# Attention by groups of four heads in 32-column array tiles, with the FFN and a hand-written order

## The chip, the cores and the metric

The kernel runs on one core of a Trainium2 chip. The metric is the device time of one execution in microseconds; the time before is the median of three runs. The profile comes from one more execution, recorded by the hardware profiler.

## The reference

The kernel computes attention with normalised queries and keys for 8 batches of 12 heads, 448 tokens and 64 channels, and then a multiplicative feed-forward network over the 3,584 tokens:

```python
q_n, k_n = rmsnorm(q, g_q), rmsnorm(k, g_k)        # over the 64 channels
scores = q_n @ k_n.transpose(0, 1, 3, 2) / sqrt(64)
attn = exp(scores - max); attn = attn / attn.sum(-1)
x = (attn @ v).transpose(0, 2, 1, 3).reshape(3584, 768)
out = (((x @ w1) * (x @ w2)) @ w3) @ w_out          # w1, w2 768x1024, w3 1024x1024, w_out 1024x768
```

Inputs and output are float32; the kernel works in bfloat16 with float32 sums. The product of w3 and w_out is formed once (W34), so that the second half of the network is one product.

## The kernel before

The unit of the attention is a pair of heads of one batch: 48 pairs. Tokens are cut into four blocks of 112. For each pair `S1_load` (L129) issues three loads on SP's queue, `S2_prep` (L143) squares q and k on POOL, sums on DVE (L151), forms the inverse root with Ln and Exp on ACT (L155, L157) and scales on DVE (L160, L167, L175), and casts v (L184). `S3_transpose_q` and `S3_transpose_k` (L189, L202) transpose on TensorE through PSUM; the transposed q is padded with zeros so that each head has its own 128 rows, half of them zero (POOL's memsets, L196 and L197).

`S4_scores` (L212) computes the scores of one head with keys on the PSUM partitions: two matmuls of 448 columns and one Exp of 896 columns on ACT (L228), twice per head. `S5_pv` (L234) takes blocks of the probabilities as weights, 112 by 112, and streams the 65 columns of v and of a column of ones: 16 matmuls per head, followed by a reciprocal and a multiplication on DVE. `S6_xT` (L259) transposes the result on TensorE into xT, 128 channels by 448 tokens.

`FFN1_chunk` (L273) runs 6 matmuls of 448 columns with w1 and 6 with w2, copies one sum on ACT (L290) and multiplies on DVE (L300). `FFN2_chunk` (L302) runs two sets of 8 matmuls of 384 columns, copies on ACT (L315) and issues two stores. `W34_chunk` (L102) forms one of eight row blocks of W34: eight transposes, each with its own copy, then two sets of 8 matmuls of 384 columns.

The order is that of the program: each engine takes its instructions in the order in which the loop over pairs (L352) issues them. The chunks of W34, FFN1 and FFN2 wait in one `chunk_queue`, and three to five are put between the steps of a pair (`nslots`, L360 to L365). The FFN of a batch enters the queue when its sixth pair is done (`tail`, L328). PSUM holds two buffers for scores (two banks each), two for `pv`, and two (`mm_psum`, L55) that the transposes, the FFN and W34 share. The weights are loaded by POOL's queue with a cast to bfloat16: w_out and w3 first, then w1 and w2 in two pieces per pair (`emit_wdma`, L97).

Of the kernel before, what the change touches and what calls it, by code (L numbers as in the profile page):

```python
# [13 lines left out]
AF = mybir.ActivationFunctionType  # L14


@with_exitstack
def kernel(
# [13 lines left out]
    nc = tc.nc  # L32

    B, H, S, D = q.shape
    NP = 112
    J = S // NP
    NPAIR = H // 2
    NPAIRS_TOTAL = B * NPAIR
    DM = moe_w1.shape[0]
    DFF = moe_w1.shape[1]  # L40
    CM = DM // 128
    CF = DFF // 128
    NH = DM // 2
# [12 lines left out]

    ident = const.tile([128, 128], BF)
    make_identity(nc, ident)

    gq_sb = const.tile([1, D], FP)  # L60
    nc.sync.dma_start(out=gq_sb, in_=g_q.unsqueeze(0))
    gk_sb = const.tile([1, D], FP)
    nc.sync.dma_start(out=gk_sb, in_=g_k.unsqueeze(0))
    gprod = const.tile([1, D], FP)
    nc.vector.tensor_tensor(out=gprod, in0=gq_sb, in1=gk_sb, op=MULT)
    gprod2 = const.tile([1, D], FP)
    nc.vector.tensor_scalar(
        out=gprod2, in0=gprod, scalar1=0.125, scalar2=None, op0=MULT
    )
    ones_row = const.tile([1, NP], FP)  # L70
    nc.vector.memset(ones_row, 1.0)
    g_bcast = const.tile([NP, D], BF)
    g_ps = mm_psum.tile([NP, D], FP, tag="mm")
    nc.tensor.matmul(out=g_ps, lhsT=ones_row, rhs=gprod2, start=True, stop=True)
    nc.vector.tensor_copy(out=g_bcast, in_=g_ps)
    eps_t = const.tile([NP, 1], FP)
    nc.vector.memset(eps_t, 1e-6)

    w1s = const.tile([128, CM, DFF], BF)
    w2s = const.tile([128, CM, DFF], BF)  # L80
    w34s = const.tile([128, CF, DM], BF)
    w3s = wstage.tile([128, CF, DFF], BF)
    w_outs = wstage.tile([128, CF, DM], BF)
    w3T = wstage.tile([128, CF, DFF], BF)

    def _load(dst, srcw, c, np_=128):
        nc.gpsimd.dma_start(
            out=dst[:, c, :],
            in_=srcw.rearrange("(c p) f -> p c f", p=np_)[:, c, :],
        )  # L90

    wdma_queue = []
    for c in range(CM):
        wdma_queue.append(lambda c=c: _load(w1s, moe_w1, c))
        wdma_queue.append(lambda c=c: _load(w2s, moe_w2, c))

    def emit_wdma(n):  # L97
        for _ in range(n):
            if wdma_queue:
                wdma_queue.pop(0)()  # L100

    def W34_chunk(fc):  # L102
        for gc in range(CF):
            tps = mm_psum.tile([128, 4, 112], BF, tag="mm")
            tview = tps.rearrange("a b c -> a (b c)")[:, 0:128]
            nc.tensor.transpose(
                tview, w3s[:, fc, gc * 128 : (gc + 1) * 128], ident
            )
            nc.vector.tensor_copy(
                out=w3T[:, gc, fc * 128 : (fc + 1) * 128], in_=tview  # L110
            )
        for nh in range(2):
            wps = mm_psum.tile([128, NH], FP, tag="mm")
            for gc in range(CF):
                nc.tensor.matmul(
                    out=wps,
                    lhsT=w3T[:, gc, fc * 128 : (fc + 1) * 128],
                    rhs=w_outs[:, gc, nh * NH : (nh + 1) * NH],
                    start=(gc == 0),
                    stop=(gc == CF - 1),  # L120
                )
            nc.scalar.copy(out=w34s[:, fc, nh * NH : (nh + 1) * NH], in_=wps)

    out_r = out.rearrange("(b p j) n -> b j p n", b=B, j=J)
    pairs = [(b, m) for b in range(B) for m in range(NPAIR)]
    st = [dict() for _ in range(NPAIRS_TOTAL)]
    xT_tiles = {}

    def S1_load(i):  # L129
        b, m = pairs[i]  # L130
        s = st[i]
        s["q_sb"] = qkv_pool.tile([NP, 2, J, D], FP, tag="q", name="q_sb")
        s["k_sb"] = qkv_pool.tile([NP, 2, J, D], FP, tag="k", name="k_sb")
        s["v_sb"] = qkv_pool.tile([NP, 2, J, D], FP, tag="v", name="v_sb")
        for t_sb, src in ((s["q_sb"], q), (s["k_sb"], k), (s["v_sb"], v)):
            nc.sync.dma_start(
                out=t_sb.rearrange("p hh j d -> p hh (j d)"),
                in_=src[b, 2 * m : 2 * m + 2].rearrange(
                    "hh (p j) d -> p hh (j d)", j=J
                ),  # L140
            )

    def S2_prep(i):  # L143
        s = st[i]
        q_sb, k_sb, v_sb = s["q_sb"], s["k_sb"], s["v_sb"]
        sq = att_pool.tile([NP, 2, 2, J, D], BF, tag="sq")
        nc.gpsimd.tensor_tensor(out=sq[:, 0], in0=q_sb, in1=q_sb, op=MULT)  # L147
        nc.gpsimd.tensor_tensor(out=sq[:, 1], in0=k_sb, in1=k_sb, op=MULT)  # L148
        ssq = att_pool.tile([NP, 2, 2, J], BF, tag="ssq")
        with nc.allow_low_precision(reason="ssq in bf16 is fine"):  # L150
            nc.vector.tensor_reduce(  # L151
                out=ssq, in_=sq, axis=mybir.AxisListType.X, op=ADD
            )
        lnv = att_pool.tile([NP, 2, 2, J], FP, tag="lnv")
        nc.scalar.activation(out=lnv, in_=ssq, func=AF.Ln, bias=eps_t, scale=1.0 / D)  # L155
        alpha = att_pool.tile([NP, 2, 2, J], FP, tag="alpha")
        nc.scalar.activation(out=alpha, in_=lnv, func=AF.Exp, scale=-0.5)  # L157
        s["alpha"] = alpha
        qtmp = att_pool.tile([NP, J, 2, D], BF, tag="qtmp")
        nc.vector.tensor_tensor(  # L160
            out=qtmp.transpose([0, 2, 1, 3]),
            in0=q_sb,
            in1=alpha[:, 0].unsqueeze(3).broadcast_to([NP, 2, J, D]),
            op=MULT,
        )
        qs = att_pool.tile([NP, J, 2, D], BF, tag="qs")
        nc.vector.tensor_tensor(  # L167
            out=qs,
            in0=qtmp,
            in1=g_bcast.unsqueeze(1).unsqueeze(1).broadcast_to([NP, J, 2, D]),  # L170
            op=MULT,
        )
# [16 lines left out]
    def S3_transpose_q(i):  # L189
# [3 lines left out]
        for j in range(J):  # L193
            nc.tensor.transpose(qT_ps[:, j, :], qs[:, j], ident[0:NP, 0:NP])  # L194
# [216 lines left out]
```

## Time and profile before

| | |
|---|---|
| time, median of 3 runs | 608.8 us (601.33 to 610.04) |
| span of the profiled execution | 605.5 us; it is the only time on its page |
| TensorE matmuls (PE) | busy 502.2 us, 83% of the span |
| ACT | busy 368.6 us, 61% |
| DVE | busy 320.4 us, 53% |
| POOL | busy 166.4 us, 27% |

The busy time of PE counts each matmul from its start to its modelled end, and matmuls follow each other before they end; how fast they follow one another is read from the chain of waits, where a run of matmuls has its true length.

### The profile page before, as it was taken

What the parts mean: (1) busy time and instruction counts of PE and PEld (TensorE: products, weight loads), DVE (VectorE), ACT (ScalarE), POOL (GpSimd) and SP (SyncE); (2) the same over time, 40 slices, a digit from 0 to 9 for tenths busy, and PEclk for the clock granted to TensorE, in tenths of its full rate; (3) what the DMA queues carried; (4) which work ended last, traced back from release to release, by engine and by line L of the source; (5) the groups of instructions that cost most, each with busy time, mean ns of one, the idle gap of its engine ahead of it and who ended that gap; (6) DMA issues with size and microseconds to landing.
All of it is one profiled execution on the core that took longest, in us unless ns stands there. A gap on an engine that the chain in (4) does not pass through costs nothing. (4 is left out here: it accounts for less than half of the span.)

```text
span 605.5 us, 10322 instructions
## 1 busy us (share of the span) xinstructions
PE 502.2 (83%) x3970; PEld 343.9 (57%) x3970; DVE 320.4 (53%) x757; ACT 368.6 (61%) x520; POOL 166.4 (27%) x267
## 2 busy tenths in 40 slices
PE   0366787989878887899888987899978887999897
PEld 0244454746665566656665565656665566767655
DVE  0546655986456555655356544756446544643120
ACT  0367346785677775765577676865667776545322
POOL 3674222432223222322223222423223211100000
PEclk9977899999968998889878899989968998899899
DMA  9997111422423123222332123312423123001103
GB/s 198 249 238 163 45 47 31 122 67 75 137 58 92 47 80 110 86 62 66 108 87 85 54 69 114 93 62 64 140 58 92 47 59 94 17 1 47 47 0 92
DMA packets 46725, 51.53 MB, mean 85 GB/s; under 512 B 3668, under 2 KB 44116, under 8 KB 46676
## 3 DMA queue, kind: packets, MB, share of 16 engines
q1 hardware_dynamic: 42756, 44.05, 24.8%
q0 software_dynamic: 3920, 6.82, 6.1%
q8 instruction: 31, 0.51, 0.3%
q14 instruction: 18, 0.15, 0.1%
HBM read 46.66 MB, written 11.01 MB: 95 GB/s over the span
## 5 line engine op out<-in xcount | busy, mean ns | idle before, releaser
L228 ACT ACTIVATE attnT<-scp 112x896 bf16<-112x896 f32 x192 | 167.9, 917 | 58.3 <-PE scp L221 56.9
L243 PE MATMUL pv<-v_aug,attnT 112*112 112x65 bf16 x1536 | 113.6, 227 | 23.3 <-ACT attnT L228 23.3
L243 PEld LDWEIGHTS <-attnT 112*112 112x112 bf16 x1536 | 109.1, 146 | 41.1 <-ACT attnT L228 26.5
L221 PE MATMUL scp<-qsT_pad,ksT 128*112 128x448 bf16 x384 | 112.9, 404 | 23.1 <-ACT attnT L228 22.7
L308 PE MATMUL po<-w34s,abT 128*112 128x384 bf16 x512 | 89.4, 329 | 0.0
L293 PE MATMUL pb<-xTb,w2s 128*128 128x448 bf16 x336 | 79.9, 378 | 0.0
L282 PE MATMUL pa<-xTb,w1s 128*128 128x448 bf16 x336 | 77.8, 370 | 0.3
L300 DVE TENSOR_TENSOR abT<-pb,a_sb 128x448 bf16<-128x448 f32 x64 | 39.8, 622 | 66.8 <-PE pb L293 45.3
L308 PEld LDWEIGHTS <-abT 128*112 128x112 bf16 x512 | 65.6, 131 | 16.2
L221 PEld LDWEIGHTS <-ksT 128*112 128x112 bf16 x384 | 47.7, 146 | 44.1 <-ACT attnT L228 23.0
L290 ACT CAST a_sb<-pa 128x448 bf16<-128x448 f32 x64 | 33.9, 530 | 61.7 <-PE pa L282 61.1
L151 DVE TENSOR_REDUCE ssq<-sq 112x16 bf16<-112x1024 bf16 x48 | 58.1, 1213 | 25.2 <-POOL sq L148 23.9
L148 POOL TENSOR_TENSOR sq<-k_sb 112x512 bf16<-112x512 f32 x48 | 52.6, 1095 | 56.4 <-DMA k_sb<-in_k_dram 55.6
L147 POOL TENSOR_TENSOR sq<-q_sb 112x512 bf16<-112x512 f32 x48 | 51.8, 1079 | 57.4 <-DVE ssq L151 47.0
L315 ACT COPY o_sb<-po 112x384 f32<-112x384 f32 x64 | 30.0, 480 | 58.1 <-PE po L308 58.1
L155 ACT ACT_TABLE_LOAD x44 | 56.5, 1283 | 10.9 <-DVE ssq L151 9.1
L293 PEld LDWEIGHTS <-w2s 128*128 128x128 bf16 x384 | 39.8, 104 | 40.9 <-issue 9.7
L196 POOL MEMSET qsT_pad<- 64x448 bf16 x48 | 22.4, 466 | 123.6 <-PE scp L221 90.6
L282 PEld LDWEIGHTS <-w1s 128*128 128x128 bf16 x384 | 37.3, 103 | 33.4 <-issue 7.3
L160 DVE TENSOR_TENSOR qtmp<-q_sb,alpha 112x512 bf16<-112x512 f32 x48 | 33.2, 692 | 34.5 <-ACT alpha L157 34.5
L198 DVE COPY qsT_pad<-qT_ps 64x448 bf16<-64x448 bf16 x48 | 18.2, 379 | 61.5 <-PE qT_ps L194 61.5
L194 PE MATMUL qT_ps<-ident,qs 112*128 112x112 bf16 x192 | 20.4, 226 | 32.7 <-DVE qs L167 19.8
(45 smaller groups left out, 496.5 us busy)
## 6 DMA issues: line engine op xcount, KB each, us to landing
q_sb<-in_q_dram SPq DMA_DIRECT2D x48, 224.0 KB, 2.6
k_sb<-in_k_dram SPq DMA_DIRECT2D x48, 224.0 KB, 2.8
v_sb<-in_v_dram SPq DMA_DIRECT2D x48, 224.0 KB, 3.0
out_dram<-o_sb SPq DMA_DIRECT2D x64, 168.0 KB, 2.2
w3s<-in_moe_w_dram POOLq DMA_DIRECT2D x8, 256.0 KB, 11.3
w_outs<-in_moe_w_out_dram POOLq DMA_DIRECT2D x1, 1536.0 KB, 15.5
w1s<-in_moe_w_dram POOLq DMA_DIRECT2D x6, 256.0 KB, 7.3
w2s<-in_moe_w_dram POOLq DMA_DIRECT2D x6, 256.0 KB, 8.1
```

The lines of the kernel that those rows point to most:

```text
L147: nc.gpsimd.tensor_tensor(out=sq[:, 0], in0=q_sb, in1=q_sb, op=MULT)
L148: nc.gpsimd.tensor_tensor(out=sq[:, 1], in0=k_sb, in1=k_sb, op=MULT)
L151: nc.vector.tensor_reduce(out=ssq, in_=sq, axis=mybir.AxisListType.X, op=ADD)
L155: nc.scalar.activation(out=lnv, in_=ssq, func=AF.Ln, bias=eps_t, scale=1.0 / D)
L221: nc.tensor.matmul(out=scp[:, u, 0:S], lhsT=ksT[:, 2 * t + u, :], rhs=qsT_pad[:, hh].rearrange("d j p -> d (j p)"), start=True, stop=True,)
L228: nc.scalar.activation(out=attnT[:, hh, 2 * t : 2 * t + 2, :], in_=scp[:, :, 0:S], func=AF.Exp,)
L243: nc.tensor.matmul(out=pv[:, jq, :], lhsT=attnT[:, hh, jk, jq * NP : (jq + 1) * NP], rhs=v_aug[:, jk, hh, :], start=(jk == 0), stop=(jk == ...
L282: nc.tensor.matmul(out=pa, lhsT=w1s[:, c, fi * 128 : (fi + 1) * 128], rhs=xT_b[:, c, :], start=(c == 0), stop=(c == CM - 1),)
L290: nc.scalar.copy(out=a_sb, in_=pa)
L293: nc.tensor.matmul(out=pb, lhsT=w2s[:, c, fi * 128 : (fi + 1) * 128], rhs=xT_b[:, c, :], start=(c == 0), stop=(c == CM - 1),)
L300: nc.vector.tensor_tensor(out=abT[:, fi, :], in0=pb, in1=a_sb, op=MULT)
L308: nc.tensor.matmul(out=po, lhsT=abT[:, fi, j * NP : (j + 1) * NP], rhs=w34s[:, fi, nh * NH : (nh + 1) * NH], start=(fi == 0), stop=(fi == ...
```

## The change

The kernel is rewritten around the same computation.

- A unit of attention is four heads (a quad, 24 of them). Keys come in blocks of 128: three full blocks per head, and the last 64 keys of two heads share a block, so a quad has seven units (`NU`), each with one Exp of 128 partitions by 896 columns on ACT.
- `qk_exp` computes a unit with eight matmuls of 448 columns: each uses 64 rows and 32 columns of the array (`tile_position`), so no zero padding is needed.
- `pv_set` takes v (32 of its 64 channels) as the weights, 128 rows by 32 columns, for four heads side by side, and streams the probabilities, 448 columns. The result is xT itself, so `S6_xT` is gone. A third set with ones as the weights gives the sums; ACT turns them into reciprocals by Ln and Exp, and DVE multiplies.
- `narrow` replaces each 128-column matmul of FFN1, FFN2 and W34 by four matmuls with 32 columns of weights each, which stream the same columns.
- FFN2 works on token blocks of 128 over two batches (7 blocks of 896 tokens), and DVE copies its result.
- The squares move from POOL to ACT for all quads (`N_SQ_ACT = 24`). One table set with Ln, Exp, Square and copies is loaded once.
- q and k of quads 0 to 4 are transposed on TensorE, those of quads 5 to 23 by a DMA transpose on SP's queue, two per quad.
- v is loaded by POOL's queue with a cast to bfloat16, four DMAs per quad; the q and k loads are cut in two along the partitions.
- `mm_psum` has four buffers; `pv` shares them.
- The order is written out in slots of two units (84 of them): scores, one set of `pv`, a share of the FFN queue, transposes, and the preparation of later quads at slots given by tables. Filling matmuls of zeros (`warm`) run at the start. The steps of W34 lie in slots 1 to 13, and the FFN of a batch is queued after its third quad.

```diff
...
-    NP = 112
-    NPAIR = H // 2
+    NP = 128
+    J = -(-S // NP)
+    NF = S // NP
+    REST = S - NF * NP
+    SPLIT = REST * J
+    NU = 2 * NF + 1
+    HQ = 4
+    NQB = H // HQ
+    NQ = B * NQB
...
+    qkT_pool = ctx.enter_context(tc.tile_pool(name="qkT", bufs=3))
     att_pool = ctx.enter_context(tc.tile_pool(name="att", bufs=2))
+    sc_psum = ctx.enter_context(tc.tile_pool(name="sc_ps", bufs=2, space=PSUM))
+    mm_psum = ctx.enter_context(tc.tile_pool(name="mm_ps", bufs=4, space=PSUM))
...
+    N_PE_T = 5
+    N_SQ_ACT = 24
+    W34_EV = 'DA'
+    W34_NARROW = True
+    WARM = (16, 2, 11, 3, 5, 0)
+    LAG = 8
+    UNITS = 3.0
+    V_COST = 0.4
+    V_AHEAD = 2
+    MOVE = 2
+    LOADS_0 = ['w0', 'w3', 'w1', 'o0', 'w2']
+    LOADS_1 = ['w4', 'v0', 'w7', 'w6', 'w5', 'v1', 'o1', 'v2']
+    GATE = ('q', 2)
+    QK1_AT = 0
+    SHIFT = [0, -1, -1, -1, -3, -3, -3]
+    PREP_1 = {'sq0': -3, 'red0': -6, 'sq1': -6, 'red1': -3, 'alpha': -8, 'sc0': -3, 't0': -2, 'sc1': -2, 't1': 0}
+    PREP = {'load': -7, 'sq0': -5, 'red0': -5, 'sq1': -4, 'red1': -4, 'alpha': -3, 'sc0': -3, 't0': -1, 'sc1': -2, 't1': -1}
+    W34_SLOTS = {1: 2, 2: 1, 3: 2, 4: 3, 5: 1, 6: 1, 7: 3, 8: 1, 9: 1, 10: 2, 11: 2, 12: 3, 13: 2}
...
+                for p0, p1, nj, t0, t1 in halves:
+                    eng.dma_start(
+                        out=t_sb[p0:p1, h0 : h0 + n, 0:nj, :].rearrange(
+                            "p h j d -> p h (j d)"
+                        ),
+                        in_=src[b, HQ * m + h0 : HQ * m + h0 + n, t0:t1].rearrange(
+                            "h (p j) d -> p h (j d)", j=nj
+                        ),
+                    )
...
+    def prep_sq(i, pr, on_act=False):
+        s = st[i]
+        if pr == 0:
+            s["ssq"] = prep_pool.tile([NP, 2, HQ, J], FP, tag="ssq", name="ssq")
+        sq = prep_pool.tile([NP, 2, 2, J, D], FP, tag="sq", name="sq")
+        s["sq", pr] = sq
+        hs = slice(2 * pr, 2 * pr + 2)
+        for t, src in enumerate((s["q"], s["k"])):
+            if on_act:
+                nc.scalar.activation(out=sq[:, t], in_=src[:, hs], func=AF.Square)
+            else:
+                nc.gpsimd.tensor_tensor(
+                    out=sq[:, t], in0=src[:, hs], in1=src[:, hs], op=MULT
                 )
...
+        qks = prep_pool.tile([NP, 2, J, 2, D], BF, tag="qks", name="qks")
         nc.vector.tensor_tensor(
+            out=qks[:, 0],
             in0=qtmp,
+            in1=g_b.unsqueeze(1).unsqueeze(1).broadcast_to([NP, J, 2, D]),
             op=MULT,
         )
         nc.vector.tensor_tensor(
+            out=qks[:, 1].transpose([0, 2, 1, 3]),
+            in0=s["k"][:, hs],
+            in1=alpha[:, 1, hs].unsqueeze(3).broadcast_to([NP, 2, J, D]),
             op=MULT,
         )
+        if pe:
+            s["qks", pr] = qks
+        else:
+            issued.add(("t", i, pr))
+            nc.sync.dma_start_transpose(
+                out=s["qkT"][:, pr].rearrange("d t (j p) -> d (t j) p", p=NP),
+                in_=qks.rearrange("p t j h d -> p (t j h d)"),
+            )
+    def prep_pe_transpose(i, pr):
+        s = st[i]
+        issued.add(("t", i, pr))
+        qks = s.pop(("qks", pr))
+        ps = mm_psum.tile([128, 2, S], BF, tag="mm", name="qkT_ps")
+        for t in range(2):
+            for j in range(J):
+                n = NP if j < NF else REST
+                nc.tensor.transpose(
+                    ps[:, t, j * NP : j * NP + n], qks[0:n, t, j], ident[0:n, 0:n]
+                )
+        nc.vector.tensor_copy(out=s["qkT"][:, pr, :, 0:S], in_=ps)
+    def qk_exp(n):
+        i, g = divmod(n, NU)
+        s = st[i]
+        if g == 0:
+            s["P"] = p_pool.tile([NP, HQ, NF, S], BF, tag="P", name="P")
+            s["Pr"] = p_pool.tile([NP, 2, S], BF, tag="Pr", name="Pr")
+        qkT = s["qkT"]
+        sc = sc_psum.tile([NP, 2, 512], FP, tag="sc", name="sc")
+        for c0 in range(0, NP, 32):
+            if g < 2 * NF:
+                pr, blk = divmod(g, NF)
+                k0 = blk * NP + c0
+            else:
+                pr = c0 // REST
+                k0 = NF * NP + c0 % REST
+            assert ("t", i, pr) in issued
             for u in range(2):
                 nc.tensor.matmul(
+                    out=sc[c0 : c0 + 32, u, 0:S],
+                    lhsT=qkT[u * D : (u + 1) * D, pr, 1, k0 : k0 + 32],
+                    rhs=qkT[u * D : (u + 1) * D, pr, 0, 0:S],
                     start=True,
                     stop=True,
+                    tile_position=(u * D, c0),
                 )
+        if g < 2 * NF:
+            dst = s["P"][:, 2 * pr : 2 * pr + 2, blk, :]
+        else:
+            dst = s["Pr"]
+        nc.scalar.activation(out=dst, in_=sc[:, :, 0:S], func=AF.Exp)
+    def pv_set(i, kind):
+        s = st[i]
+        b, m = divmod(i, NQB)
+        ps = mm_psum.tile([128, S], FP, tag="mm", name="pv")
+        for j in range(J):
+            for h in range(HQ):
+                if kind:
+                    w = s["v"][:, h, j, (kind - 1) * HALF : kind * HALF]
+                else:
+                    w = ones[:, 0 if j < NF else 1 + h // 2, :]
                 nc.tensor.matmul(
+                    out=ps[h * HALF : (h + 1) * HALF, :],
+                    lhsT=w,
+                    rhs=s["P"][:, h, j, :] if j < NF else s["Pr"][:, h % 2, :],
+                    start=(j == 0),
+                    stop=(j == J - 1),
+                    tile_position=(0, h * HALF),
                 )
+        if kind == 0:
+            s["r"] = att_pool.tile([128, S], FP, tag="r", name="r")
+            nc.scalar.activation(out=s["r"], in_=ps, func=AF.Ln)
+            nc.scalar.activation(out=s["r"], in_=s["r"], func=AF.Exp, scale=-1.0)
+            return
+        if b not in xT:
+            xT[b] = x_pool.tile([128, CM, S], BF, tag="xT", name="xT")
         nc.vector.tensor_tensor(
+            out=xT[b][:, 2 * m + kind - 1, :], in0=ps, in1=s["r"], op=MULT
+        )
+        if kind == 2:
+            s.clear()
+            if m == NQB - 1:
+                push_ffn(b)
+    def narrow(ps, n, lhsT, rhs, start, stop):
+        for h in range(4):
+            nc.tensor.matmul(
+                out=ps[32 * h : 32 * h + 32, 0:n],
+                lhsT=lhsT[:, 32 * h : 32 * h + 32],
+                rhs=rhs,
+                start=start,
+                stop=stop,
+                tile_position=(0, 32 * h),
+            )
...
+    def ffn1_a(b, fi):
+        ps = mm_psum.tile([128, 512], FP, tag="mm", name="pa")
+        for c in range(CM):
+            narrow(
+                ps, S, w1s[:, c, fi * 128 : (fi + 1) * 128], xT[b][:, c, :],
+                c == 0, c == CM - 1,
+            )
+        a_sb = ffn_pool.tile([128, S], BF, tag="a_sb", name="a_sb")
+        nc.scalar.copy(out=a_sb, in_=ps[:, 0:S])
+        a_tiles[b, fi] = a_sb
...
+        for fi in range(CF):
+            narrow(
+                ps, NH, abT[bp][:, fi, t * 128 : (t + 1) * 128],
+                w34s[:, fi, nh * NH : (nh + 1) * NH], fi == 0, fi == CF - 1,
+            )
...
+    def push_ffn(b):
+        assert not wq
+        for fi in range(CF):
+            fillers.append(lambda b=b, fi=fi: ffn1_a(b, fi))
+            fillers.append(lambda b=b, fi=fi: ffn1_b(b, fi))
+        bp, odd = divmod(b, 2)
+        for t in range(3, 7) if odd else range(3):
+            for nh in range(2):
+                fillers.append(lambda bp=bp, t=t, nh=nh: ffn2(bp, t, nh))
...
+        nc.scalar.preload_act_table_set("natural_log_exp_and_others")
...
+        for t in range(max(todo) + 1):
+            if t == QK1_AT:
+                load_qk(1)
+            mine = agenda.pop(t, [])
...
+            for n in range(2 * t, min(2 * t + 2, NQ * NU)):
+                qk_exp(n)
...
+            old = len(fillers)
+            for i, kind in todo.get(t, []):
+                pv_set(i, kind)
+            for n, part in mine:
+                if part == "v":
+                    load_v(n)
+            for _ in range(4):
+                if wq:
+                    wq.pop(0)()
+            if t in W34_SLOTS:
+                for _ in range(W34_SLOTS[t]):
+                    if w34q:
+                        w34q.pop(0)()
+            elif not w34q:
+                last = min([p for p in pushes if p >= t] or [t])
+                every = sum(room(z) for z in range(t, last + 1))
+                fill(int(old * room(t) / every + 0.5))
+            for n, part in mine:
+                if part[0] == "t":
+                    prep_part(n, part)
+            for n, part in mine:
+                if part[0] != "t" and part not in ("load", "v"):
+                    prep_part(n, part)
+        fill(len(fillers))
```

## Rows read from the trace of the kernel before

**Rows 1.** The page: busy time of engines, then the granted TensorE clock in 40 slices.

```profile
PE 502.2 (83%) x3970; PEld 343.9 (57%) x3970; DVE 320.4 (53%) x757; ACT 368.6 (61%) x520; POOL 166.4 (27%) x267
...
PEclk9977899999968998889878899989968998899899
```

**Rows 2.** Busy time by stage: stage, length, engines (x instructions), granted clock, DMA share, GB/s.

```profile
0.00:60.00 60.00, 26.49 (x195) 18.16 (x196) 27.50 (x67) 27.50 (x38) 34.07 (x58) 0.88 0.97 212
60.00:115.00 55.00, 43.97 (x371) 29.11 (x371) 33.55 (x107) 29.51 (x45) 13.55 (x21) 0.91 0.19 53
115.00:571.00 456.00, 401.12 (x3243) 278.31 (x3242) 253.99 (x576) 303.45 (x422) 118.82 (x188) 0.92 0.26 76
571.00:605.50 34.50, 30.60 (x164) 18.29 (x164) 5.39 (x9) 8.09 (x16) 0.00 (x0) 0.95 0.14 40
```

**Rows 3.** Source line 282, the first 130 us: first matmuls of FFN1.

```profile
L282 PE MATMUL pa<-xT,w1s x24: 349/352/356, 115.1 to 129.2; 128*128 128x448 bf16 x24
```

**Rows 4.** The chain of waits at its end: start, length in us, what.

```profile
543.06 0.76 PE scp L221 x4
...
558.47 0.91 PE pv L243 x18
...
571.35 1.82 PE pa L282 x6
...
588.93 1.13 PE pa L282 x6
590.06 1.14 PE pb L293 x6
591.20 10.41 PE po L308 x64
```

**Rows 5.** Timeline at 306 us, TensorE: four transposes in a row.

```profile
306.01 0.36 PE L207 MATMUL kT_ps<-ident,kb 112*128 112x112 bf16 x4
```

**Rows 6.** Groups of instructions by line: busy us, mean ns, then idle time before.

```profile
L228 ACT ACTIVATE attnT<-scp 112x896 bf16<-112x896 f32 x192 | 167.9, 917 | 58.3 <-PE scp L221 56.9
...
L155 ACT ACT_TABLE_LOAD x44 | 56.5, 1283 | 10.9 <-DVE ssq L151 9.1 <-PEq L395 0.7
...
L228 ACT ACT_TABLE_LOAD x34 | 43.6, 1283 | 0.6
...
L290 ACT CAST a_sb<-pa 128x448 bf16<-128x448 f32 x64 | 33.9, 530 | 61.7 <-PE pa L282 61.1
...
L151 DVE TENSOR_REDUCE ssq<-sq 112x16 bf16<-112x1024 bf16 x48 | 58.1, 1213 | 25.2 <-POOL sq L148 23.9 <-ACT lnv L155 1.3
...
L160 DVE TENSOR_TENSOR qtmp<-q_sb,alpha 112x512 bf16<-112x512 f32 x48 | 33.2, 692 | 34.5 <-ACT alpha L157 34.5
...
L167 DVE TENSOR_TENSOR qs<-qtmp,g_bcast 112x512 bf16<-112x512 bf16 x48 | 20.9, 435 | 0.0
...
L300 DVE TENSOR_TENSOR abT<-pb,a_sb 128x448 bf16<-128x448 f32 x64 | 39.8, 622 | 66.8 <-PE pb L293 45.3 <-ACT a_sb L290 20.0 <-PE scp L221 1.3
...
L315 ACT COPY o_sb<-po 112x384 f32<-112x384 f32 x64 | 30.0, 480 | 58.1 <-PE po L308 58.1
```

**Rows 7.** The page's DMA queues (packets, MB, share), HBM traffic, and issues to landing.

```profile
q1 hardware_dynamic: 42756, 44.05, 24.8%
q0 software_dynamic: 3920, 6.82, 6.1%
...
HBM read 46.66 MB, written 11.01 MB: 95 GB/s over the span
...
q_sb<-in_q_dram SPq DMA_DIRECT2D x48, 224.0 KB, 2.6
...
w_outs<-in_moe_w_out_dram POOLq DMA_DIRECT2D x1, 1536.0 KB, 15.5
```

**Rows 8.** Timeline, the first scores on TensorE.

```profile
26.05 1.70 PE L221 MATMUL scp<-qsT_pad,ksT 128*112 128x448 bf16 x4
```

**Rows 9.** Waits of SP's queue: who waited for whom, us in total, times, longest.

```profile
SPq L136 <- DVE kb L175: 166.5, 42, 9.1
```

More of the change, by code (lines that the diff above doesn't have):

```diff
@@ L14 @@
 AF = mybir.ActivationFunctionType
+AX = mybir.AxisListType.X
+PSUM = bass.MemoryType.PSUM
 @with_exitstack
@@ L70 @@
[L70 to L82, printed above, removed]
@@ new lines @@
+    gp_row = const.tile([1, D], BF, name="gp_row")
+    ones_row = const.tile([1, NP], BF, name="ones_row")
+    g_b = const.tile([NP, D], BF, name="g_b")
+    ident = const.tile([128, 128], BF, name="ident")
+    ones = const.tile([NP, 3, HALF], BF, name="ones")
+    warm_t = const.tile([128, 512], BF, name="warm_t")
+    gate = const.tile([NP, 1], FP, name="gate")
+    eps_t = const.tile([NP, 1], FP, name="eps_t")
+    qk_bufs = [
+        [const.tile([NP, HQ, J, D], FP, name=n + str(z)) for n in ("q_sb", "k_sb")]
+        for z in range(3)
+    ]
@@ new lines, with load_qk @@
+    v_bufs = [
+        const.tile([NP, HQ, J, D], BF, name="v_sb" + str(z)) for z in range(4)
+    ]
+    halves = ((0, REST, J, 0, SPLIT), (REST, NP, NF, SPLIT, S))
+    st = [dict() for _ in range(NQ)]
+    issued = set()
+    xT = {}
+    abT = {}
+    def load_qk(i, split=1, k_eng=None):
+        b, m = divmod(i, NQB)
+        s = st[i]
+        s["q"], s["k"] = qk_bufs[i % 3]
+        n = HQ // split
+        for h0 in range(0, HQ, n):
+            for t_sb, src, eng in (
+                (s["q"], q, nc.sync),
+                (s["k"], k, k_eng or nc.sync),
+            ):
+                for p0, p1, nj, t0, t1 in halves:
[7 more added lines that the diff above has]
+                    )
@@ L87, in _load, with load_w12 @@
+    def load_w12(dst, src, h, half):
+        issued.add(("w12", h, half))
         nc.gpsimd.dma_start(
-            out=dst[:, c, :],
-            in_=srcw.rearrange("(c p) f -> p c f", p=np_)[:, c, :],
-        )
[L92 to L107, printed above, removed]
-            )
[L109 to L122, printed above, removed]
@@ L143, in S2_prep @@
-    def S2_prep(i):
-        s = st[i]
[L145 to L159, printed above, removed]
+            out=dst[h * HALF : (h + 1) * HALF, half::2, :],
@@ L252, in S5_pv @@
         nc.vector.tensor_tensor(
[L253 to L255 removed]
+            out=abT[bp][:, fi, odd * S : (odd + 1) * S],
+            in0=ps[:, 0:S],
+            in1=a_tiles.pop((b, fi)),
             op=MULT,
         )
[L259 to L269 removed]
@@ L379, with ffn2 @@
-    tail(NPAIRS_TOTAL - 1)
-    emit_chunk(len(chunk_queue))
+    o_tiles = {}
+    def ffn2(bp, t, nh):
+        if nh == 0:
+            o_tiles[bp, t] = out_pool.tile([128, DM], FP, tag="o_sb", name="o_sb")
+        o_sb = o_tiles[bp, t]
+        ps = mm_psum.tile([128, 512], FP, tag="mm", name="po")
+        for fi in range(CF):
+            narrow(
+                ps, NH, abT[bp][:, fi, t * 128 : (t + 1) * 128],
+                w34s[:, fi, nh * NH : (nh + 1) * NH], fi == 0, fi == CF - 1,
+            )
+        last = (bp, t) == (B // 2 - 1, 6)
+        nc.vector.tensor_copy(out=o_sb[:, nh * NH : (nh + 1) * NH], in_=ps[:, 0:NH])
+        if nh == 0 and not last:
+            return
+        n0, n1 = (nh * NH, (nh + 1) * NH) if last else (0, DM)
+        for z, c0 in enumerate(range(t * 128, (t + 1) * 128, REST)):
+            bb, f = divmod(c0, S)
+            j, p = divmod(f, NP)
+            _, _, nj, t0, t1 = halves[p // REST]
+            r0 = (2 * bp + bb) * S
+            (nc.scalar if last and z else nc.sync).dma_start(
+                out=out[r0 + t0 : r0 + t1].rearrange("(p j) n -> j p n", j=nj)[
+                    j, :, n0:n1
+                ],
+                in_=o_sb[z * REST : (z + 1) * REST, n0:n1],
+            )
```

473 lines of the change are left out of this document (250 added, 223 removed).

## Prediction

> **What bounds the kernel now.** I first read the busy shares: TensorE is busy 83% of the span, ACT 61%, DVE 53% [rows 1]. A busy matmul is not a streaming one, so the next view is the chain of waits, where a run of matmuls has its true length: six of 448 columns last 1.13 to 1.14 us, or 189 ns each, and 64 of 384 columns last 10.41 us, or 162.7 ns each; four score matmuls last 0.76 us (190 each); 18 `pv` matmuls with a weight load of 112 columns each last 0.91 us (50.5 a pair of load and matmul) [rows 4]. 448 columns in 187 ns is 2.4 GHz. At the lower level the same six matmuls take 1.82 us and more [rows 4].
>
> Third, stages [rows 2]. Until 60 us the DMA engines are full and PE is busy 26 us; the first scores run at 26.05 us [rows 8], the first FFN1 at 115.1 us [rows 3]. From 115 to 571 us forty pairs and seven eighths of the FFN run; then come 34.5 us of FFN alone. What must the middle stream? A pair has 8 score matmuls (1.52 us), 32 `pv` (1.62) and 12 transposes, of which four take 0.36 us [rows 5], so 1.08: 4.22 us, by 40 is 169. The FFN has 768 matmuls by 189 = 145.2 and 512 by 162.7 = 83.3 us; seven eighths are 200. Together 369 of 456 us. The granted clock of 0.92 [rows 2] accounts for some 36 us of the rest, waits for 51. Where do they come from? ACT is busy 303 of these 456 us, and an Exp of scores waits behind table loads of 1283 ns: 78 on two lines alone, 100 us [rows 6]. So the stage is bound by TensorE's stream, with gaps that ACT and the order put in.
>
> **The change on TensorE.** Four 32-column matmuls (a quartet) replace one of 128. No row shows array tiles side by side. If the four overlap fully, a quartet costs what one matmul costs, 189 or 162.7 ns; if each pair of load and matmul costs what a `pv` pair does, it costs 4 x 50.5 = 202. I take 195 and 170: the pair of the rows loads 112 columns, the new one 32, so the streaming end is nearer. A score unit has eight pairs: between 189 (all eight side by side) and 8 x 50.5 = 404; I take 250, by the same reasoning.
>
> - Scores: 168 units by 250 ns = 42.0 us (31.8 to 67.9), where 384 by 190 = 73 were.
> - `pv`: 24 quads by 3 sets by 4 blocks are 288 quartets by 195 = 56.2 (54.4 to 58.2), where 1536 by 50.5 = 77.6 were. It is a swap of operands that pays for the ones with a third set.
> - FFN1: 768 quartets, 149.8 (145.2 to 155.1). FFN2: 4 x 7 x 2 x 8 = 448 quartets by 170 = 76.2 (72.9 to 90.5), where 512 matmuls took 83.3: the blocks are 128 tokens, not 112.
> - W34: 128 quartets, 21.8 (20.8 to 25.9), and 64 transposes as before.
> - Transposes: 576 by at most 90 ns = 52 us become 80, 7 us; `S6_xT` is gone.
> - Scores use tiles of 64 rows, the rest 128 rows, so each slot changes the shape twice. The rows show no change of shape. Its cost lies between nothing and the time by which one matmul outlasts its columns, 352 - 187 = 165 ns [rows 3]. I take 80: 84 slots x 2 x 80 = 13.4 us (0 to 27.7).
>
> The Trainium skill speaks against this part ("TensorEngine Tiling (Array Packing)", Key Properties): "Changing tiling mode (not just tile) drains the TensorE". If each change drains fully, by the row's 165 ns, the sum below grows by 20 x 7 x 85 ns = 12 us; nothing before shows a drain.
>
> **ACT, DVE and the queues.** Per quad ACT has seven Exps of 917 ns (6.42), Ln and Exp of 448 columns (2 x 0.53 by the copy of that size), four squares of 512 columns (about 0.53 each, 2.1) and two small activations (0.5): 10.1 us [rows 6]. Twenty quads are 202 us, and 56 copies of 530 ns make 232 in the middle, where it had 303. The table loads go, squares come. DVE per quad has two sums of 1213, two scalings of 692 + 435 + 692, and two multiplications of 622 (7.3 us, so 146), then 56 by 622 and 49 output copies by about 480 (58): 204 us. Both stay under the TensorE work below, so they cost nothing while the order keeps them fed; without that cover ACT's lead is only some 60 us. Moving the squares to ACT puts them ahead of Exps in its order: 2.1 us a quad, counted in the 10.1.
>
> The DMA transposes wait on SP's queue for the scaled q and k, and behind them stand the loads of later quads and the stores; SP already waits 166.5 us for DVE's scaling [rows 9], and loads run quads ahead. No row shows a transposing DMA. A tile of 256 KB lies between 2.6 us (a 224 KB load) and 15.5 us (the 1.5 MB of w_out, in the crowded start) [rows 7]. There are 38 of them, two in 3.5 slots or some 14 us, so they are covered up to about 7 us each. I take 2.6 to 5: nothing.
>
> **The start** is a matter of bytes. In its first 60 us the chip wrote 212 GB/s [rows 2], 12.7 MB, of which 6.8 MB are weights, read as twice that in float32 [rows 7]: 19.5 MB read, 325 GB/s. FFN1 cannot start before all of w1 and w2 is there, and they are loaded last. Weights (13.6 MB), q and k of four to six quads (3.7 to 5.5) and v of four (1.8) are 19.1 to 20.9 MB: 59 to 64 us, and I take 64. TensorE's own 14 slots are less: 4 quads by 4.65 (below), 25 to 30 of W34, 7 of transposes, about 53 us from 12 us on, in part beside the loads. This stage took 115 us before; its W34 chunks ran late and one by one.
>
> **The sum.** Start 64. The middle: a quad streams 7 x 0.25 + 12 x 0.195 + 7 x 0.08 = 4.65 us, by 20 = 93.0; seven eighths of 149.8 + 76.2 are 197.7; together 290.7. For waits and clock I add 20 us, a quarter of the 87 lost before: no table loads, four PSUM buffers where two were. That is 311. The tail: 96 quartets by 195 and 64 by 170 = 29.6, and 3.9 from the last matmul to the end, as now (601.6 to 605.5): 33.5. Sum 408.5 us as a span; the median stands 3 above the profiled span, so **411 us**, 32% less than 608.8.
>
> **Rivals.**
> 1. *Pairs bound by issue or weight loads.* Every quartet takes 202 and a unit 404. The middle is 20 x (2.83 + 2.42 + 0.56) + 7/8 x 245.6 = 331 + 20, the tail 36: 454. For it: 50.5 ns is the fastest pair shown. Against: that pair is as long as its 112 columns at 2.4 GHz (47 ns).
> 2. *The order stalls as before.* The middle loses 87 us, not 20: 478. For it: nothing in a written order follows a late DMA. Against: the loads that cause it go.
> 3. *Better than taken.* Units of 189, no cost of shape, start 59, 5 us of waits: 20 x 3.59 + 190.8 + 5 = 268, tail 31: 361.
> 4. *Tiles overlap only in part.* If each quartet leaves one pair of load and matmul uncovered, it takes 189 + 50.5 = 240 ns (213 for 384 columns). The middle is 20 x 5.19 + 244.8 + 20 = 369, the tail 41: 476. For it: a weight load must fit beside the matmul of its own tile. Against: the loads of 128 columns are hidden in the FFN rows of before. The Trainium skill has a figure on this side ("TensorE: Matmul & The Clock Gate", Measured speedup vs the span model): four tiles ran 3.07 times as fast, not four; an estimate by it is 246 ns a quartet and some 482 us, and no run here shows it yet.
> 5. *Slower: tiles run one after another.* A quartet takes 4 x 189 = 757 ns; the middle and tail hold quartets worth some 1400 of 448 columns, so the time is about 137 + 1400 x 0.757, near 1200 us. It decides from 336 ns a quartet, where the same sum is 608. For it: no row shows two matmuls streaming at once. Against it: the four use different columns of the array and write different partitions.
>
> **How the numbers follow.** Forecast (380 to 440) 0.55; rival 1 0.13; rival 2 0.10; rival 3 0.12; rival 4 0.05; rival 5 0.05. The range takes the unknown bounds, the better case down to 365, and rivals 1, 2 and most of 4: **365 to 480**. A measurement of this kernel tells about 2% from no change. Only rival 5 is slower (0.05); 0.02 lies within 2%; 0.93 is faster.
>
> **What would show it.** A run of FFN1 quartets: six in 1.13 to 1.2 us (forecast), 1.21 (rival 1), 1.5 (rival 4), 4.5 (rival 5). Scores: a unit in 0.25 us. First FFN1 at about 64 us, scores at about 12. No ACT table loads in the loop. PE's idle time in the middle ended by the DMA transpose would prove the cover wrong; by ACT, rival 2. The prediction is wrong above all if quartets don't overlap, or if the order waits on something that the old trace has no row for.

## The result and the profile after

The changed kernel takes 391.7 us (median of 4; 390.84 to 396.32) against 608.5 us: a ratio of 0.648 with a 95% interval of 0.641 to 0.655. The forecast was 411 us in a range of 365 to 480. The profiled execution has a span of 389.5 us, 216 us less than that of before.

Busy shares and the granted clock, from the page of the changed kernel, answer to [rows 1]:

```profile
PE 372.9 (96%) x8053; PEld 193.2 (50%) x8054; DVE 242.6 (62%) x398; ACT 265.5 (68%) x443; POOL 75.6 (19%) x131
...
PEclk9889999999999999999999999999999999999999
```

TensorE went from 83 to 96% of a much shorter span, at full clock nearly throughout. The stages of [rows 2], with the first two taken as one, cut at the first FFN1 matmul and at the last `pv` (columns as there):

```profile
0.00:71.50 71.50, 64.16 (x1093) 32.42 (x1098) 48.16 (x87) 50.51 (x90) 34.38 (x63) 0.95 1.09 208
71.50:354.00 282.50, 277.73 (x6276) 142.31 (x6268) 183.37 (x294) 210.77 (x346) 41.22 (x68) 1.00 0.76 138
354.00:389.50 35.50, 30.98 (x700) 18.49 (x692) 11.08 (x19) 4.26 (x8) 0.00 (x0) 0.98 0.28 69
```

The start shrank from 115 to 71.5 us, the middle from 456 to 282.5, and the tail stayed. The chain of waits shows how the new stream runs (start, length in us, what; from two stretches of the changed kernel):

```profile
206.75 1.32 PE pa L354 x24
208.07 1.14 PE pb L354 x24
209.20 0.50 PE sc L297 x16
209.71 0.87 PE pv L322 x16
210.57 1.14 PE pa L354 x24
211.71 1.14 PE pb L354 x24
212.84 0.50 PE sc L297 x16
...
348.41 0.76 PE pv L322 x16
...
374.58 10.43 PE po L354 x256
```

Twenty-four 32-column matmuls take 1.14 us, what six whole ones took in [rows 4]: a quartet costs 190 ns, four fully side by side. In FFN2, 64 quartets take 10.43 us, 163 ns each. A slot is 3.64 us long (209.20 to 212.84), made of 0.50 + 0.87 + 1.14 + 1.14 without a gap. Where `pv` follows matmuls of its own shape, its four quartets take 0.76 us (348.41); behind the scores they take 0.87, 0.11 more. Two score units at 190 ns (run 3 shows one by itself) are 0.38 us of the 0.50, 0.12 less. So at each change of tile shape 0.11 to 0.12 us are over.

By line (columns as in [rows 6]), the Exp costs what it did, with 128 instead of 112 partitions, and the new work on ACT is the squares and the Ln and Exp of the sums:

```profile
L309 ACT ACTIVATE P<-sc 128x896 bf16<-128x896 f32 x144 | 125.1, 913 | 29.4 <-PE sc L297 29.4
...
L203 ACT ACTIVATE sq<-q_sb 128x512 f32<-128x512 f32 x48 | 30.2, 630 | 0.0
...
L332 ACT ACTIVATE r<-pv 128x448 f32<-128x448 f32 x24 | 13.1, 547 | 0.2 <-PE pv L322 0.2
```

And the DMA transposes, from the view of DMA issues (count, median us to landing):

```profile
qkT<-qks SPq DMA_TRANSPOSE x38, 4.7
```

### The profile page after: what moved, and what is told of

Read it like the earlier page. It is cut to its first block, busy times and chain, and to the rows that moved or that the text cites. A ratio compares the mean times of both kernels' runs of the same rounds, so it can differ in the third digit from the quotient of the medians.

```text
span 389.5 us, 17790 instructions
## 1 busy us (share of the span) xinstructions
PE 372.9 (96%) x8053; PEld 193.2 (50%) x8054; DVE 242.6 (62%) x398; ACT 265.5 (68%) x443; POOL 75.6 (19%) x131
## 4 chain that ended last, share of the span: by engine, by line
PE 78%; DMA 9%; DVE 4%; ACT 4%; SPq 3%; issue 2%; DVEq 0%; ACTq 0%
PE pa L354 17%; PE pb L354 17%; PE po L354 14%; PE pv L322 13%; PE sc L297 9%; PE wps L354 5%; DMA out_dram<-o_sb 5%; DMA k_sb<-in_k_dram 2%; SPq L129 2%; PE qkT_ps L272 2%; DVE ssq L214 2%; ACT P L309 1%; DVE o_sb L430 1%; DMA q_sb<-in_q_dram 1%; PE w3T_ps L367 1%
## 5 line engine op out<-in xcount | busy, mean ns | idle before, releaser
L309 ACT ACTIVATE P<-sc 128x896 bf16<-128x896 f32 x144 | 125.1, 913 | 29.4 <-PE sc L297 29.4
L354 PE MATMUL pa<-xT,w1s 128*32 128x448 bf16 x1536 | 83.9, 353 | 0.7 <-DVE xT L337 0.7
L354 PE MATMUL pb<-xT,w2s 128*32 128x448 bf16 x1536 | 83.8, 352 | 0.0
L152 POOL DMA_DIRECT2D v_sb<-in_v_dram x72 | 43.8, 620 | 200.5 <-PE pv L322 174.5
L354 PE MATMUL po<-w34s,abT 128*32 128x384 bf16 x1792 | 77.5, 326 | 2.8 <-DVE o_sb L430 2.8
L214 DVE TENSOR_REDUCE ssq<-sq 128x16 f32<-128x1024 f32 (+1 forms) x50 | 58.2, 1169 | 11.6 <-ACT sq L203 11.6
L354 PEld LDWEIGHTS <-abT 128*32 128x32 bf16 x1792 | 48.1, 97 | 29.6 <-issue 3.3
L354 PEld LDWEIGHTS <-w1s 128*32 128x32 bf16 x1536 | 40.4, 97 | 34.3 <-issue 4.9
L354 PEld LDWEIGHTS <-w2s 128*32 128x32 bf16 x1536 | 41.4, 97 | 31.3
L430 DVE COPY o_sb<-po 128x384 f32<-128x384 f32 x56 | 30.5, 556 | 41.0 <-DMA out_dram<-o_sb 21.4
L297 PE MATMUL sc<-qkT 64*32 64x448 bf16 x1344 | 48.9, 357 | 1.8 <-ACT P L309 1.3
```

The lines of the kernel that those rows point to most:

```text
L152: nc.gpsimd.dma_start(out=dst.rearrange("p h j d -> p h (j d)"), in_=part.rearrange("p h j d -> p h (j d)"),)
L214: nc.vector.tensor_reduce(out=s["ssq"][:, slice(*t), hs, :], in_=sq[:, slice(*t)], axis=AX, op=ADD)
L297: nc.tensor.matmul(out=sc[c0 : c0 + 32, u, 0:S], lhsT=qkT[u * D : (u + 1) * D, pr, 1, k0 : k0 + 32], rhs=qkT[u * D : (u + 1) * D, pr, 0, 0:S],
L309: nc.scalar.activation(out=dst, in_=sc[:, :, 0:S], func=AF.Exp)
L354: nc.tensor.matmul(out=ps[32 * h : 32 * h + 32, 0:n], lhsT=lhsT[:, 32 * h : 32 * h + 32], rhs=rhs, start=start, stop=stop, tile_position=( ...
L430: nc.vector.tensor_copy(out=o_sb[:, nh * NH : (nh + 1) * NH], in_=ps[:, 0:NH])
```

## The experiments

The theory: TensorE's stream became shorter, and ACT, PSUM and the order stopped interrupting it. The rivals: the narrow matmuls themselves are the gain, or one cause alone (table loads, say) would have done. Runs 2 and 7 to 10 have one time each; the others are medians of four or five, set against the kernel before on the same chip, which took 607.5 to 609.3 us beside them.

**1. Whole matmuls in place of the FFN's and W34's quartets.**

```diff
     def narrow(ps, n, lhsT, rhs, start, stop):
-        for h in range(4):
-            nc.tensor.matmul(out=ps[32 * h : 32 * h + 32, 0:n], lhsT=lhsT[:, 32 * h : 32 * h + 32],
-                rhs=rhs, start=start, stop=stop, tile_position=(0, 32 * h))
+        nc.tensor.matmul(out=ps[:, 0:n], lhsT=lhsT, rhs=rhs, start=start, stop=stop)
```

> The changed kernel with each quartet of FFN1, FFN2 and W34 replaced by one matmul of 128 weight columns; scores and pv keep their 32-column tiles. Theory (quartets stream like one matmul, and each change of the tile shape costs about 0.115 us): the stream stays, one more change of shape per slot is added, some 84 x 0.115 = 10 us, so 398 to 404 us. Rival (the quartets of the FFN gain by themselves): the FFN slows by over 5%, 415 us or more. Rival (four instructions in place of one cost something): faster than 388.

390.3 us (ratio 0.6402, 0.6385 to 0.642): no difference from 391.7, and not the 398 to 404 of the theory. So quartets do not gain by themselves. But the cost that I expected is in the slots: the chain of this run has a slot of 3.75 us, with 0.10 us more on the first FFN sum behind `pv`:

```profile
202.90 1.24 PE pa L353 x6
204.15 1.14 PE pb L353 x6
205.28 0.50 PE sc L297 x16
205.78 0.87 PE pv L322 x16
206.65 1.24 PE pa L353 x6
```

Why the whole is not slower for it is the question of runs 4 and 5.

**2. The matmuls of a sum in another order.** The order inside the first FFN1 sum is by tile, not by term.

```diff
-        for c in range(CM):
-            narrow(ps, S, w1s[:, c, ...], xT[b][:, c, :], c == 0, c == CM - 1)
+        for h in range(4):
+            for c in range(CM):
+                nc.tensor.matmul(out=ps[32 * h : 32 * h + 32, 0:S], ..., tile_position=(0, 32 * h))
```

> The changed kernel with the 24 matmuls of each first FFN1 sum put in another order: all six of one 32-column tile, then the next tile; nothing is left out. Theory (the gain of a quartet needs four neighbours in different columns; matmuls of one tile follow each other at 189 ns): 384 quartets cost 757 instead of 189 ns, 218 us more, 605 to 612 us, as long as the kernel before. Rival (TensorE finds the overlap by itself further down its queue): under 420 us.

457.3 us: neither. The sum takes about 2.3 us (24 matmuls), not 1.14 and not 4.54 (24 by 189 ns). The timeline of TensorE in this run (start, length in us) says why; `pa` comes before `pb` in the program:

```profile
373.96 1.91 PE L393 MATMUL pa<-xT,w1s 128*32 128x448 bf16 x20
375.53 0.37 PE L354 MATMUL pb<-xT,w2s 128*32 128x448 bf16 x2
375.70 0.37 PE L393 MATMUL pa<-xT,w1s 128*32 128x448 bf16 x2
375.73 0.51 PE L354 MATMUL pb<-xT,w2s 128*32 128x448 bf16 x3
375.90 0.35 PE L393 MATMUL pa<-xT,w1s 128*32 128x448 bf16 x1
```

Matmuls of `pb` start while four of `pa` have not: TensorE starts a matmul whose columns are free ahead of an earlier one whose columns are not. So tiles overlap even when their matmuls stand one behind the other, though here only about two at a time, as 24 in 2.3 us are 97 ns each. Four neighbours in four different columns are what makes the overlap full. The Trainium skill says the opposite of one part ("TensorE: Matmul & The Clock Gate", The mechanism, under What overlaps and what doesn't: matmuls start and end strictly in program order); here they don't, and the measurement decides.

**3. Twice as many changes of shape.**

```diff
-            for n in range(2 * t, min(2 * t + 2, NQ * NU)):
+            mine_u = list(range(2 * t, min(2 * t + 2, NQ * NU)))
+            cut = 1 if t >= 14 else 2
+            for n in mine_u[:cut]:
                 qk_exp(n)
...
                 pv_set(i, kind)
+            if not todo.get(t, []):
+                fill(1)
+            for n in mine_u[cut:]:
+                qk_exp(n)
```

> The changed kernel where, from slot 14 on, the second score unit of each slot stands behind the pv set (or one FFN sum) instead of directly behind the first, so that the tile shape changes four times a slot instead of twice. Theory (a change costs about 0.115 us of stream): 70 slots x 2 x 0.115 = 16 us more, 405 to 410 us. Rival (the 0.11 us in the chain are something else, such as a wait for the Exp): within 4 us of 391.7.

409.2 us (0.6704, 0.6673 to 0.6735): 17.4 us more for about 140 further changes, 0.12 us each. The chain agrees, each score unit now carrying its own change:

```profile
206.47 0.31 PE sc L297 x8
206.79 1.25 PE pb L354 x24
208.04 1.14 PE pa L354 x24
209.17 0.31 PE sc L297 x8
```

A second unit without a change of its own adds 0.50 - 0.31 = 0.19 us, so 0.31 is 0.19 of stream and 0.12 of change. The theory holds. The Trainium skill warns that a change of tiling mode drains TensorE ("TensorEngine Tiling (Array Packing)", Key Properties); the runs agree that a change costs time. The page gives no price, and here it is 0.11 to 0.12 us.

**4. Three output tiles.**

```diff
-    out_pool = ctx.enter_context(tc.tile_pool(name="outp", bufs=2))
+    out_pool = ctx.enter_context(tc.tile_pool(name="outp", bufs=3))
```

> The changed kernel with three output tiles instead of two, so that DVE's copy of an FFN2 sum no longer waits for the store of two blocks earlier (21.4 us of such waits in nine places). Theory (TensorE streams nearly all of the middle, DVE's wait is mostly covered): 387 to 391 us. Rival (DVE's wait is passed on to TensorE, as the chain of waits shows it with 20 us on stores): 372 to 380 us.

386.1 us (0.6345, 0.6313 to 0.6377), 5.6 us faster. The wait that it removes stood in the view of waits of the changed kernel (who waited for whom, us in total, times, longest):

```profile
DVE o_sb L430 <- DMA out_dram<-o_sb: 21.4, 9, 5.2
```

In the middle of the changed kernel TensorE was idle for 4.8 of 282.5 us (the rows of the result). In this run it has no gap there, and the middle is 6 us shorter (columns as in [rows 2]):

```profile
72.20:348.70 276.50, 276.50 (x6268) 141.39 (x6264) 183.72 (x293) 210.71 (x346) 41.83 (x70) 1.00 0.79 142
```

So some 6 of DVE's 21.4 us of waiting reached TensorE (the idle time is a little less than that, as a matmul counts as busy to its modelled end). The theory's 387 to 391 is the nearer; it put the gain a little too low.

**5. Three output tiles and whole matmuls.** The edits of 1 and 4 together.

> Three output tiles (386.1 us with quartets) and one matmul of 128 weight columns in place of each quartet of FFN1, FFN2 and W34. It settles why the wide form alone was not slower although its slots in the middle are 0.11 us longer. Theory (in the changed kernel the stores held TensorE up, and a slower TensorE only waited less; without that wait the third change of shape counts): 84 x 0.1 = 8 us more than 386.1, 392 to 396 us. Rival (128-column matmuls give the time back elsewhere): 388 us or less.

389.7 us (0.641, 0.6376 to 0.6443), 3.6 us above run 4, between the two. In the profiled executions, the middle (first FFN1 to last `pv`) takes 276.5 us with quartets (72.2 to 348.7) and 283.2 with whole matmuls (71.8 to 355.0), and TensorE has no gap in either: 6.7 us for the third change of shape in 69 slots, 0.10 each. In run 1 it was hidden. TensorE is busy there for 283.3 of the 283.5 us of the middle: the changes stand where the changed kernel had its 6 us of waits, and FFN1 starts at 69.3 us instead of 71.5. The medians of runs 4 and 5 lie only 3.6 us apart. The profiled execution of run 5 is its slowest, 392.1 us, and what the others gain is not shown.

**6. The kernel before with one table set.** One line is added to the kernel before.

```diff
+    nc.scalar.preload_act_table_set("natural_log_exp_and_others")
     ident = const.tile([128, 128], BF)
```

> The kernel before with one activation table set, loaded once, that has both Ln and Exp: the 88 table loads of 1.28 us, 113 us of ACT's time, go; the recording layer places some instructions differently. Theory (table loads make most of the gaps in TensorE's stream): 40 to 87 us less, 520 to 570 us. Rival (the gaps come from the two shared PSUM buffers, the late W34 chunks and the order): 590 us or more.

525.2 us (0.8647, 0.8596 to 0.8699): 82 us of the 217 come from this alone. Its stages, to be set beside [rows 2]:

```profile
60.00:115.00 55.00, 48.25 (x418) 31.75 (x417) 38.36 (x112) 24.79 (x43) 17.06 (x26) 0.94 0.21 60
115.00:490.00 375.00, 354.14 (x3154) 252.28 (x3152) 242.22 (x557) 203.75 (x342) 113.03 (x182) 0.99 0.30 89
490.00:526.40 36.40, 31.53 (x178) 19.13 (x178) 6.53 (x13) 8.30 (x17) 0.00 (x0) 0.95 0.13 39
```

ACT's busy time falls from 303 us in the 456 of the middle to 204 in 375, and the clock rises from 0.92 to 0.99. From the first FFN1 (106.3 us) to the last `pv` (491.2) are 385 us. The prediction counted 369 us of stream for this stage, but it took the transposes from a timeline, where a length runs to the modelled end of the last matmul. In the chain of waits four of them take 0.20 us, not 0.36 (this run):

```profile
446.69 0.20 PE qT_ps L194 x4
```

With this, the matmuls that the trace has in this stage stream for 352 us at the times of [rows 4], and 33 us of waits are left; in the 375 us of the row above TensorE is idle for 21. So most of what goes on from here is a shorter stream. One reservation: the kernel before is put in order by the recording layer, engine by engine and not quite as the program stands (the section on it takes the order for the program's), and with the new line it places some instructions differently. The two traces show another order in the first 71 us alone. From there on every engine has the same order in both, so the 71 us by which the middle is shorter (456 to 385) are not the order's; the 9 us of the start can be both.

**7. The changed kernel with table loads.** The preloading line is deleted.

```diff
-        nc.scalar.preload_act_table_set("natural_log_exp_and_others")
```

> The changed kernel without the preloaded set: 99 table loads instead of one, 126 us more on ACT, which is busy 265 of 389 us now. Theory (ACT's cover is gone): ACT becomes the bound with 391 us of work and TensorE waits, 430 to 470 us. Rival (ACT's idle time takes the loads): under 405 us.

466.1 us. ACT becomes the bound. Busy time by engine on the page of this run, then the shares of the chain of waits, of this run and of the changed kernel:

```profile
PE 395.3 (85%) x8054; PEld 202.4 (44%) x8054; DVE 244.5 (53%) x398; ACT 390.4 (84%) x541; POOL 75.4 (16%) x131
...
ACT 47%; PE 34%; issue 8%; DVE 6%; DMA 4%; SPq 1%; ACTq 0%; DVEq 0%
...
PE 78%; DMA 9%; DVE 4%; ACT 4%; SPq 3%; issue 2%; DVEq 0%; ACTq 0%
```

The busy shares of the two engines are alike, but the chain runs over ACT for 47% of the span, where it was 4%. In the middle (86.5 to 428.6 us) ACT is busy for 313 of 342 us; the last 36 us leave it little to do. Table loads are worth nearly as much here (74 us) as in the kernel before (82).

**8. Two shared PSUM buffers.**

```diff
-    mm_psum = ctx.enter_context(tc.tile_pool(name="mm_ps", bufs=4, space=PSUM))
+    mm_psum = ctx.enter_context(tc.tile_pool(name="mm_ps", bufs=2, space=PSUM))
```

> The changed kernel with two instead of four shared PSUM buffers for FFN, W34, pv and transposes. Theory (with two, each sum waits for the copy of the one before last behind Exps and squares in ACT's and DVE's order): 420 us or more. Rival (two are enough, the copy of 0.53 to 0.62 us fits beside the next sum of 1.14 us): under 400 us.

431.7 us: 40 us of the gain hang on the two further buffers, for which the two that `pv` had to itself made room.

**9. All transposes on TensorE.**

```diff
-    N_PE_T = 5
+    N_PE_T = 24
```

> The changed kernel with q and k of all 24 quads transposed on TensorE; the 38 DMA transposes go. Theory (TensorE's stream is the bound, so what the DMA transposes take off it counts in full): 38 sets of eight transposes at 0.81 us, 31 us more, 415 to 425 us. Rival (the transposes by DMA crowd the queues and stores, so their removal gives much of it back): under 405 us.

419.3 us, 27.6 more, for 38 sets. In the middle TensorE has no gap, and 306.6 us are 30 more than in run 4, for 36 sets at 0.81 us, or 29: the stream counts in full. The whole is less since the changed kernel's 6 us of waits go, and the start grows by 4. Transposes by DMA were covered (4.7 us each, while a quad lasts some 14 us), and no wait of TensorE in the changed kernel is ended by one.

**10. W34 with one of its eight terms.**

```diff
-        for gc in range(CF):
+        for gc in range(1):
```

> The changed kernel with W34 summed over the first of its eight terms only (the other seven are left out), which takes 112 quartets or 18 us from TensorE's first 70 us. Theory (TensorE's stream sets the start of FFN1 at 71.5 us, and the last piece of w1 lands at 64): FFN1 starts at 64 to 66 us, 383 to 387 us. Rival (the bytes or ACT set it): FFN1 at 70 us or later, over 389 us. Rival (nothing but TensorE): FFN1 at 54 us, 374 us or less.

382.7 us, just under the 383 to 387 of the theory, and FFN1 starts at 64.2 us (the view of the line, then the timeline of TensorE):

```profile
L354 PE MATMUL pa<-xT,w1s x192: 349/353/364, 64.2 to 89.4; 128*32 128x448 bf16 x192
...
64.16 0.36 PE L354 MATMUL pa<-xT,w1s 128*32 128x448 bf16 x4
65.09 1.13 PE L354 MATMUL pa<-xT,w1s 128*32 128x448 bf16 x20 [0.57 <-DMA w1s<-in_moe_w_dram]
```

Behind the first four matmuls TensorE waits for the bytes of the weights, for 0.6 us: the last piece of w1 is issued at 55.4 us in this run and takes 9.5 us in its chain of waits, to 65 us. So the bytes are there at 65, and with all of W34, TensorE is the later one by 6 to 7 us. It came to FFN1 only 7 us earlier with 18 us less of stream, and is busy for 50 of the first 64 us: in the slots before it waited, in part for ACT and DVE. That the bytes alone set the 64.2 is not shown.

**11 and 12. Two steps further.** Run 11 has three output tiles and whole matmuls for W34 alone; run 12 adds `N_PE_T = 3`.

```diff
-    W34_NARROW = True
+    W34_NARROW = False
...
-    N_PE_T = 5
+    N_PE_T = 3
```

> Three output tiles, and 128-column matmuls for W34 alone; FFN1 and FFN2 keep their quartets. W34 lies between transposes that use the whole array, so fewer changes of shape are left in the start. Theory: 2 to 3 us less than 386.1, 382 to 385 us. Rival (the start is set by bytes, or a change between whole-array and 32-column forms is free): 385.5 to 388 us.

384.8 us (0.6307, 0.6263 to 0.6351): inside the expected 382 to 385, but its interval overlaps that of run 4, so the last step is open. Runs 4 and 11 are faster than the changed kernel, and run 11 is the fastest version here that leaves nothing out.

> As the run before it, and q and k of quads 3 and 4 transposed by DMA instead of on TensorE: four sets of eight transposes at 0.81 us, 3 us, leave a stage that TensorE's stream bounds. Theory: 3 us less than the run before it, 379 to 383 us. Rival (in the start the DMA engines are full, and the transposes come late or delay the weights): equal to the run before it or slower.

406.5 us (0.6673, 0.6626 to 0.672), 22 us slower than run 11. The theory fell, and the loss is in the start: FFN1 begins at 92.2 us, not 71.3, and the middle has no gap. The transposes of quad 3 land in the crowded start; the waits of this run say

```profile
PEld L297 <- DMA qkT<-qks: 20.3, 2, 16.7
PE sc L297 <- DMA qkT<-qks: 19.6, 2, 16.4
```

and the tile's own view gives their landing times (us, least, median, most):

```profile
DMA to landing us min/median/max: 3.0/5.0/18.6
```

A transpose that takes 4.7 us in the middle takes up to 18.6 beside the weights, and SP's queue spends 10 us on issuing two of them. TensorE takes 1.6 us for the same. Whether the full DMA engines or SP's queue make them late is not separated.

## Why the prediction was right

The direction, the size and the mechanism hold: quartets overlap, the stream of the middle becomes shorter, and TensorE is kept fed. The trace has 138 units, 248 `pv` and 672 FFN1 quartets in the middle, at 0.19 us, 368 FFN2 quartets at 0.163 and 138 changes of shape at 0.115: 277 us, where the kernel before streamed 352 (run 6). The gap-free middle of run 4, 276.5 us, agrees. The 19 us between the forecast span of 408.5 and the 389.5 measured come from sizes, stage by stage. The middle was 28.5 us too long and the other two stages 9.5 too short, so it is luck that the total is off by 19 alone.

- *Start*, 64 forecast, 71.5 measured. The step "TensorE's own 14 slots are less" failed. The bytes were sized right: w1's last piece lands at about 65 us (run 10). But 53 us of work from 12 us on would end at 65, not before 64, and the first scores ran at 13 us, with work that left no long gaps only from 22.7 on. From there TensorE is busy for 47.7 of 48.8 us: it was the bound, by 6 to 7 us.
- *Middle*, 311 forecast, 282.5 measured. A score unit takes 190 ns, not the 250 taken (140 units: 8.4 us less); the quartets take 190 and 163, not 195 and 170 (7.3 less); a change of shape takes 0.115 us, not 0.08 (4.9 more); 24 of the FFN2 quartets stand in the tail (3.9 less); waits take 6 us, not 20 (14 less). That makes 282. The 20 were a quarter of 87 us, which rest on the 369; with 352, 104 us were lost before. A pair of load and matmul has no fixed price of 50.5 ns: eight pairs now start in 190 ns, 24 each. This fits a load of 112 columns as the reason for the 50.5, but the new pairs also run side by side, and no run separates the two.
- *Tail*, 33.5 forecast, 35.5 measured: 80 FFN2 quartets stand in it, where 64 were taken (2.6 us; the forecast's 392 in the middle and 64 here are eight more than the 448). The median lies 2.2 above the span, where 3 was taken.

Rival 1 (pairs bound by issue) and rival 4 (partial overlap, 240 ns) fall by the 1.14 us of 24 matmuls; the 3.07 of the Trainium skill ("TensorE: Matmul & The Clock Gate", Measured speedup vs the span model), a row on four row tiles, is not met by these column tiles, which are four times as fast in a steady stream (1.14 us where 24 by 189 ns are 4.54). Rival 5 falls too; run 2 shows that even tile after tile this sum costs 66 us, not hundreds. Rival 2 (the order stalls) falls, with 6 us of waits, though runs 7 and 8 show how near it is, 74 us for the table loads and 40 for two PSUM buffers. Rival 3 was the closest, with its 190 ns and few waits, but it left out the price of the shape changes and the start.

Where did the 216 us of span go? Run 6 splits them. One table set takes 79 us off the old structure (605.5 to 526.4), mostly in the middle, with clock and waits. From there to the changed kernel the middle falls from 385 us (106.3 to 491.2 in run 6) to 282.5: 75 of these 102 are stream, 352 to 277, and 27 are waits, 33 to 6. Of the stream, scores fall from 62 to 26 us, `pv` from 66 to 47, transposes from 24 to none and FFN2 from 73 to 60 (some 4 only by moving to the tail), against 16 for changes of shape. The start falls from 106 to 71.5, 35 us; that W34 lies beside the first quads, by order, is the likely reason, but no run puts it back. The parts overlap and can't be added up: table loads and fewer PSUM buffers, put back one at a time (runs 7 and 8), each cost the changed kernel tens of microseconds. What more PSUM buffers alone would give the kernel before is not tested.

The cover that was costed at nothing held for the DMA transposes and for ACT, which had 211 us in the middle (232 forecast). DVE had 183 (204), but its copies waited for stores to land (4.3 to 6.0 us each in the chain of waits), and that is what cost the 6 us that run 4 gives back. Left open is how much of the order's tables matters; the runs change single parts of it. No run puts back the old form of the scores or of `pv`: what they save is read from the chains of waits.

## What to carry to other kernels

First take away what interrupts TensorE (activation sets that alternate, too few PSUM buffers), then count its stream: once the gaps are gone, each microsecond of stream counts in full, here 29 us of transposes as 30 (run 9). Array tiles are as fast as the whole array if neighbours in the queue use different columns; they pay only where they save stream (half-empty rows, a swap of operands), not by being narrow. A change of tile shape has a price, so pieces of one shape belong together, and a cover that holds in the middle (a DMA transpose) must be checked in the crowded start.

## What the runs showed of the hardware

- TensorE starts matmuls out of program order when their columns are free (run 2): with six matmuls of one tile in a row, a sum of 24 takes about 2.3 us, half of what one tile after the other would.
- A change between 64-row and 128-row tiles, and between 32 and 128 columns, costs 0.10 to 0.12 us each (runs 1, 3 and 5).
- A DMA transpose of 256 KB lands in 3.0 to 6.7 us in the changed kernel, and in up to 18.6 us beside the weight loads (run 12).
- The granted clock was higher where TensorE had fewer gaps: 0.915 over the kernel before (busy 83%), 0.977 with one table set (88%), 0.989 after the change (96%).
